# The first microseconds of a fused layernorm, state-space and gated feed-forward kernel: first tile loaded in halves, parameters on another queue, transposed tiles evicted in halves

## The chip, the cores and the metric

The kernel runs on one core of a Trainium2 chip. The metric is device time in microseconds; 179.80 is the median of three runs of the kernel before. One execution was also profiled; "the profile" is the page made of it and "the trace" is what can be asked of it beyond the page. The names of the engines are those of the profile: PE is TensorE's matmuls and PEld its weight loads, DVE is VectorE, ACT is ScalarE, POOL is GpSimd, SP is SyncE, which here only issues DMAs. ScalarE issues a few DMAs as well.

## The reference

The input x has 2048 tokens of 512 channels. Three things are summed:

```python
xn = _layernorm(x, axis=-1)
return x + _A_ref(xn, ...) + _B_ref(xn, ...)

# _A_ref: a diagonal complex state-space layer with 512 states
dt = jnp.exp(log_dt)
Lam_bar = jnp.exp(dt * Lam)
B_bar = ((Lam_bar - 1.0) / Lam)[:, None] * Bmat
Bu = jnp.einsum("bld,pd->blp", x + 0j, B_bar)
h = Lam_bar[None, :] * h + Bu[:, t, :]          # over all tokens t
y = 2.0 * jnp.einsum("blp,dp->bld", hseq, Cmat).real + x * Dskip[None, None, :]

# _B_ref: a gated feed-forward layer, 512 -> 1376 -> 512
return (_gelu(x @ w_gate) * (x @ w_up)) @ w_down
```

All inputs and the output are bf16.

## The kernel before

The 2048 tokens are 16 tiles of 128 and 4 blocks of 512. A tile has its 128 tokens on the partitions. It is normalised (statistics, then "centring": subtract the mean, multiply by the reciprocal root) and then transposed, so that channels lie on the partitions for the matmuls. In block 0, "the lead", TensorE transposes: four 128x128 transposes for a tile go into one PSUM bank (`TR_lead`, L594), and ScalarE copies the bank into the transposed array XNT, called its eviction (L597). Tile 0 alone is centred, transposed and evicted in two halves of two transposes each. The other blocks are transposed by DMA (`TR`, L640).

TensorE's work then is, block by block: gate and up projections (`gu_mm`, L772, on 128 rows of the hidden dimension at a time; `lead_gates_first`, L608, and `lead_mm` do the first two such row groups tile by tile in the lead), the state-space input B (`bu_mm`, L715), the down projection (L846) and the state-space output C (L857), which adds to the same bank. The state-space recurrence runs on VectorE: the input is rotated by tables of sines and cosines (L743 to L748), scanned (L754) and rotated back (`CHAIN`).

The decay parameters log_dt, Lambda_re and Lambda_im are three loads of 1 KB (`ld_param`, L475). Each is transposed on TensorE (`TR_par`, L617), and ScalarE takes the exponentials and copies from the PSUM bank it went to (`decay`, L653 to L659); VectorE makes the phases of these (L660 to L665) and the tables' arguments (L670 to L674).

Statistics of the lead's tiles are two VectorE operations (L530, L531). The reciprocal root is two ScalarE operations for tiles 0, 1 and 3 (L565, L566) and two GpSimd operations for tile 2 (L550, L551). `LN_lead` pins VectorE's order: statistics of tiles 0 and 1, both half centrings of tile 0 (L559), statistics of tile 2, and in between the centring of tile 1 (L546), then tile 3's statistics and the centrings of tiles 2 and 3.

Order of the work. Every operation is registered with the buffers that it reads and writes and an estimated duration. TensorE and SyncE run their operations in the order of registration. For VectorE, ScalarE and GpSimd a list scheduler picks the order by estimated times and due times, except for what `S.pin` fixes: pinned operations of an engine come first, in the order given. Waits are then generated: every operation waits for the semaphores of what it depends on, and an engine runs strictly in its order. A DMA issue is an operation of the engine that issues it.

Before any data is there, TensorE runs filler matmuls (`warm_pe`, L873): two of 128 columns and eight of 512, and one of 128 between tile 0's transposes and the first gate matmuls. The lead's order on TensorE and the pinned order on ScalarE are these:

```python
evT = [TR_lead(0)]
TR_par(0)
TR_par(1)
warm_pe(1, 128, 3)
lead_gates_first()
evT.append(TR_lead(1))
lead_mm((0, 1), 0, 1, (1,))
lead_mm((0,), 1, 2)
evT.append(TR_lead(2))
...
S.pin(*prm, g0, u0, ldln, *rs[0], *rs[1], *evT[0], exps[0], *evT[1], *rs[3], *evT[2], cps[1], *exps[1:3], *evT[3],
      *exps[3:], cps[0], gelu0)
```

ScalarE's queue thus issues log_dt, Lambda_re and the first columns of the gate and up weights (g0, u0) before it loads its first table (ldln). SyncE's queue issues the four lead tiles one by one, Lambda_im, the two transposing loads of B (L479), and the rest of the weights and tiles.

Of the kernel before, what the change touches and what calls it, by code (L numbers as in the profile page):

```python
# [9 lines left out]
ALU = mybir.AluOpType  # L10
# [308 lines left out]
def d_pe(n_list):  # L319
    return sum(max(62.0, n / 2.4 + 2.5) for n in n_list)  # L320
# [10 lines left out]
def build(nc, ins, out):  # L331
    with ExitStack() as es:
# [175 lines left out]

        POOL(lambda e: e.memset(NHALF.ap, -0.5), 100, [], [NHALF], "const")
        POOL(lambda e: e.memset(EPS.ap, EPS_LN), 100, [], [EPS], "const")  # L510
        POOL(lambda e: e.iota(IOT.ap, [[1, 128]], base=0, channel_multiplier=-1), 300, [], [IOT], "iota")
        POOL(lambda e: e.iota(IOTJ.ap, [[1, 512]], base=0, channel_multiplier=0), 600, [], [IOTJ], "iotj")
        ZWs = [Buf("ZWa", "sb", ZW.lo, ZW.lo + 256, ZW.ap[:, 0:128]), Buf("ZWb", "sb", ZW.lo + 256, ZW.hi, ZW.ap[:, 128:512])]
# [11 lines left out]

        GATE = {"gelu": []}

        def stats(tt):
            b, j = divmod(tt, 4)
            return [V(lambda e: e.bn_stats(ST[tt].ap, X[tt].ap), 640, [X[tt]], [ST[tt]], "bnst", slack=4000.0),  # L530
                    V(lambda e: e.bn_aggr(MVt[b][j].ap, ST[tt].ap), 100, [ST[tt]], [MVt[b][j]], "bnag", slack=4000.0)]  # L531
# [17 lines left out]
        def rsqrt(dst, var, r, n):  # L549
# [4 lines left out]
                for h in range(2)]  # L554
        XNT0h = [Buf("XNT0h%d" % h, "xnt", 0.5 * h, 0.5 * (h + 1)) for h in range(2)]

# [44 lines left out]

        def lead_gates_first():
            for h in range(2):
                def f(e, h=h):
                    ins_ = None
                    for dk in range(2 * h, 2 * h + 2):
                        for k in range(2):
                            ins_ = e.matmul(PS[2 * k][:, 0:128], WG.ap[:, dk, 128 * k:128 * k + 128], XNT[0].ap[:, dk, 0:128],  # L608
                                            start=(dk == 0), stop=(dk == KD - 1))
                    return ins_  # L610
                PE(f, d_pe([128] * 4), [WGc[0], XNT0h[h]], [bank_part(2 * k, 0, 512) for k in range(2)], "GU0")

        PPB = (5, 5, 4)
        PP = [PSH[PPB[i]][:, KP * i:KP * (i + 1)] for i in range(3)]

# [3 lines left out]
        def LN(b, on_act=True):  # L619
            for tt in range(4 * b, 4 * b + 4):  # L620
                sums(tt) if on_act else stats(tt)
            if on_act:
                rsqrt(RQb[b], SSQb[b].ap, [SSQb[b]], 4)
                POOL(lambda e: e.tensor_scalar(NRQb[b].ap, SUMb[b].ap, -1.0 / D, None, ALU.mult), 250, [SUMb[b]], [NRQb[b]], "nrq")
                POOL(lambda e: e.tensor_tensor(NRQb[b].ap, NRQb[b].ap, RQb[b].ap, ALU.mult), 1500, [NRQb[b], RQb[b]], [NRQb[b]], "nrq")  # L625
            else:
                rsqrt(RQb[b], MV[b].ap[:, :, 1], [MV[b]], 4)
            for j in range(4):
                tt = 4 * b + j
# [4 lines left out]
                else:  # L634
                    center(tt)

# [15 lines left out]
        def decay():  # L652
            exps = [ACT(lambda e: e.activation(DTB.ap, PP[0], ACTF.Exp), 200, [BANK[5]], [DTB], "exp_dt")]  # L653
            for s in range(KP):
                exps.append(ACT(lambda e, s=s: e.activation(PA[RRr].ap[:, s:s + 1], PP[1][:, s:s + 1], ACTF.Exp,
                                                            scale=DTB.ap[:, s:s + 1]),
                                200, [BANK[5], DTB], [A.sub(PA[RRr], "RR_%d" % s, s)], "exp_a"))
            c = [ACT(lambda e: e.activation(LRE.ap, PP[1], ACTF.Copy), 200, [BANK[5]], [LRE], "par"),
                 ACT(lambda e: e.activation(LIM.ap, PP[2], ACTF.Copy), 200, [BANK[4]], [LIM], "par")]  # L659
            d = [V(lambda e: e.tensor_tensor(pa(TH), DTB.ap, LIM.ap, ALU.mult), D_TINY, [DTB, LIM], [PA[TH]], "th"),  # L660
# [73 lines left out]
        def CHAIN(b):  # L734
# [146 lines left out]
        def preload(tag, fn=lambda e: e.preload_act_table(ACTF.Gelu_apprx_tanh)):  # L881
# [120 lines left out]
```

## Time and profile before

| | |
|---|---|
| median of three runs | 179.80 us (179.71 to 180.05) |
| the profiled execution | 179.66 us |
| its span, first to last instruction | 177.9 us |
| TensorE busy | 174.1 us, 98% of the span |
| VectorE busy | 161.8 us, 91% |
| ScalarE busy | 103.5 us, 58% |
| GpSimd busy | 9.5 us, 5% |
| first filler matmul, first transposes, first B matmul | 0.98, 4.90, 10.62 us |

A line of the chain is "start us, us, what": the chain is followed back from the last instruction, at each step to what released it or to the instruction before it on its engine. A line of a timeline is "start us, us, engine line op out<-in xcount [idle before <-releaser]", where neighbours of one line are merged. The time of a matmul in a group's row contains its drain; where matmuls follow each other, the distance of their starts is the time that each costs. A line of DMA issues ends with the us from issue to landing. Times of single instructions and packets are read from the same trace.

### The profile page before, as it was taken

The page shows a single profiled execution, that of the slowest core. Times are in us where ns is not written, and L with a number is a line of the kernel's source. Part 1 is how long each engine was busy: PE and PEld are TensorE (multiplying, and loading weights), DVE is VectorE, ACT ScalarE, POOL GpSimd, SP SyncE. Part 2 cuts the span into 40 slices and gives each one's busy share as a digit, 9 for nine tenths or more (in the row PEclk, how much of TensorE's full clock was granted, in tenths as well). Part 3 has the DMA queues.
Part 4 walks back from the last instruction along what each step waited for, and adds up shares of the span by engine and source line. Part 5 has one row for each costly group of instructions (what it writes and reads, how often), then busy time and mean ns, then how long its engine had stood idle before and what let it go on. Part 6 is the DMA issues. An engine that isn't in the chain of part 4 may idle for free.

```text
span 177.9 us, 2417 instructions
## 1 busy us (share of the span) xinstructions
PE 174.1 (98%) x881; PEld 81.9 (46%) x881; DVE 161.8 (91%) x249; ACT 103.5 (58%) x199; POOL 9.5 (5%) x21
## 2 busy tenths in 40 slices
PE   7999999999999999999999999999999999999994
PEld 2664444444444444444444444444444444444463
DVE  5799999998999989999999999999988999999631
ACT  3699999899998999396667500047867610000000
POOL 2100210000000601400000000000000000000000
PEclk9999999999999999999999999999999999999999
DMA  5999635995000022232000000110000000002020
GB/s 141 261 283 345 198 61 131 314 188 132 0 0 0 4 60 58 88 90 58 4 2 0 0 0 0 61 63 0 0 0 0 4 0 0 0 29 88 4 88 30
DMA packets 25267, 12.38 MB, mean 70 GB/s; under 512 B 15432, under 2 KB 25256, under 8 KB 25256
## 3 DMA queue, kind: packets, MB, share of 16 engines
q1 hardware_dynamic: 24184, 11.70, 25.6%
q10 hardware_dynamic: 1072, 0.53, 1.2%
q8 instruction: 7, 0.11, 0.2%
q14 instruction: 4, 0.03, 0.1%
HBM read 6.46 MB, written 2.10 MB: 48 GB/s over the span
## 4 chain that ended last, share of the span: by engine, by line
PE 95%; DVE 1%; DMA 1%; ACT 0%; issue 0%
PE PS L772 39%; PE PS L846 21%; PE PS L857 16%; PE PS L715 16%; PE PS L804 2%; DMA arena<-in_A_x_dram 1%; PE PS L820 1%; DVE arena L530 1%; PE PS L594 1%; PE PS L608 0%; ACT arena L597 0%; DVE arena L864 0%; DVE arena L531 0%; DVE arena L559 0%; PE PS L617 0%
## 5 line engine op out<-in xcount | busy, mean ns | idle before, releaser
L772 PE MATMUL PS<-arena 128*128 128x512 bf16 (+1 forms) x360 | 70.1, 354 | 0.1
L772 PEld LDWEIGHTS PS<-arena 128*128 128x128 bf16 x360 | 32.8, 98 | 36.6 <-ACT arena L811 0.8
L846 PE MATMUL PS<-arena 128*128 128x512 bf16 (+3 forms) x187 | 39.0, 366 | 0.0
L754 DVE TENSOR_TENSOR_SCAN arena<-arena 128x512 bf16<-128x512 f32 x32 | 38.6, 1251 | 0.0
L857 PE MATMUL PS<-arena 128*128 128x512 bf16 (+1 forms) x136 | 28.6, 366 | 0.0
L715 PE MATMUL PS<-arena 128*128 128x512 bf16 x128 | 28.3, 379 | 0.0
L780 ACT ACTIVATE arena<-PS 128x512 bf16<-128x512 f32 x40 | 23.8, 595 | 6.5 <-PE PS L772 4.9
L846 PEld LDWEIGHTS PS<-arena 128*128 128x128 bf16 (+1 forms) x187 | 18.3, 98 | 20.0
L724 ACT ACTIVATE arena<-PS 128x512 bf16<-128x512 f32 x26 | 15.1, 598 | 20.0 <-PE PS L715 19.9
L782 ACT ACTIVATE arena<-PS 128x512 bf16<-128x512 f32 x40 | 23.9, 596 | 4.9 <-PE PS L772 4.5
L857 PEld LDWEIGHTS PS<-arena 128*128 128x128 bf16 x136 | 13.3, 98 | 14.4
L715 PEld LDWEIGHTS PS<-arena 128*128 128x128 bf16 x128 | 12.5, 98 | 14.8
L784 DVE TENSOR_TENSOR arena<-arena 128x512 bf16<-128x512 bf16 x40 | 16.2, 420 | 2.9 <-ACT arena L782 2.2
L743 DVE TENSOR_TENSOR arena<-arena 128x4096 bf16<-128x4096 bf16 x8 | 18.3, 2286 | 0.1
L744 DVE TENSOR_TENSOR arena<-arena 128x4096 bf16<-128x4096 bf16 x8 | 18.3, 2283 | 0.0
L864 DVE TENSOR_TENSOR arena<-PS,arena 128x512 bf16<-128x512 f32 (+1 forms) x17 | 10.8, 652 | 6.6 <-PE PS L857 6.3
L834 DVE TENSOR_TENSOR arena<-arena 128x512 f32<-128x512 bf16 x16 | 10.8, 689 | 0.4
L745 DVE TENSOR_TENSOR arena<-arena 128x2048 bf16<-128x2048 bf16 x8 | 9.8, 1220 | 0.2
L631 ACT ACTIVATE arena<-arena 128x512 bf16<-128x512 bf16 x8 | 6.0, 803 | 2.5 <-POOL arena L625 2.5
L833 DVE TENSOR_TENSOR arena<-arena 128x512 bf16<-128x512 bf16 x16 | 6.4, 417 | 0.0
L530 DVE BATCH_NORM_STATS2 arena<-arena 128x6 f32<-128x512 bf16 x8 | 5.2, 680 | 1.1 <-DMA arena<-in_A_x_dram 1.1
L707 DVE SCALAR_TENSOR_TENSOR arena<-arena 128x512 bf16<-128x512 bf16 x8 | 5.7, 745 | 0.3 <-ACT arena L705 0.3
(74 smaller groups left out, 101.6 us busy)
## 6 DMA issues: line engine op xcount, KB each, us to landing
out_dram<-arena SPq DMA_DIRECT2D x15, 128.0 KB, 1.7
arena<-in_A_x_dram SPq DMA_DIRECT2D x3, 512.0 KB, 7.2
arena<-in_B_w_down_dram SPq DMA_DIRECT2D x1, 1280.0 KB, 6.8
arena<-in_B_w_gate_dram SPq DMA_DIRECT2D x2, 384.0 KB, 6.4
arena<-in_B_w_up_dram SPq DMA_DIRECT2D x2, 384.0 KB, 7.0
arena<-in_A_x_dram SPq DMA_DIRECT2D x4, 128.0 KB, 2.8
arena<-in_B_w_gate_dram SPq DMA_DIRECT2D x1, 352.0 KB, 8.5
arena<-in_B_w_up_dram SPq DMA_DIRECT2D x1, 352.0 KB, 7.9
```

Of the source, the lines that this page charges most:

```text
L715: ins_ = e.matmul(PS[bank][:, c0:c1], BBT[c].ap[:, dk, 128 * s:128 * (s + 1)], XNT[b].ap[:, dk, c0:c1], start=(dk == 0), stop=(dk == KD - 1))
L724: return ACT(lambda e: e.activation(ss.ap, PS[bank][:, :], ACTF.Copy), d_act(512), [BANK[bank]], [ss], "evBu", slack=1500.0)
L743: V(lambda e: e.tensor_tensor(TB.ap, ssb.ap, sin4, ALU.mult), d_dve_tt2x(4096), [ssb, SINT], [TB], tag)
L744: V(lambda e: e.tensor_tensor(TA.ap, ssb.ap, cos4, ALU.mult), d_dve_tt2x(4096), [ssb, COST], [TA], tag)
L754: V(lambda e, g=g, rb=rb, init=init: e.tensor_tensor_scan(g.ap, rb, g.ap, init, ALU.mult, ALU.add), d_dve_scan(512), [g, PA[RRr]] + ([CARc ...
L772: ins_ = e.matmul(PS[bank][0:m, c0:c1], W.ap[:, dk, 128 * ft:128 * ft + m], XNT[b].ap[:, dk, c0:c1], start=(dk == 0), stop=(dk == KD - 1))
L780: g = ACT(lambda e: e.activation(GG[kk].ap[0:m, :], PS[bg][0:m, :], ACTF.Gelu_apprx_tanh), d_act(512), [BANK[bg]], [GG[kk]], "gelu", after ...
L782: u = ACT(lambda e: e.activation(UPB[kk].ap[0:m, :], PS[bu][0:m, :], ACTF.Copy), d_act(512), [BANK[bu]], [UPB[kk]], "evU", slack=1500.0)
L784: h = V(lambda e: e.tensor_tensor(HTt[k2][ft].ap[0:m, :], GG[kk].ap[0:m, :], UPB[kk].ap[0:m, :], ALU.mult), d_dve_tt2x(512), [GG[kk], UPB[ ...
L834: V(lambda e: e.tensor_tensor(XD[tt % 4].ap, X[tt].ap, XN[tt].ap, ALU.add), d_dve_1x(512), [X[tt], XN[tt]], [XD[tt % 4]], "xd")
L846: ins_ = e.matmul(o_, HTt[k2][ft].ap[0:m, tok], WD.ap[0:m, ft, c0:c1], start=(ft == 0), stop=False)
L857: ins_ = e.matmul(o_, SSc[k3][s][c].ap[:, tok], CT[c][s].ap[:, c0:c1], start=False, stop=(s == KP - 1 and c == 1))
```

## The change

The first x tile is loaded as two halves of 64 rows: the upper one, with a new name X0B, is the first issue of ScalarE's queue, and the lower one the first of SyncE's; tile 0's statistics wait for both. The three parameter loads move to GpSimd's queue, and GpSimd's start is pinned: the small iota, two constants, the three loads, then the large iota. VectorE's pinned order puts the centring of tile 1 before the statistics of tile 2.

In the lead, tile 1 and tile 2 are now transposed into two banks and evicted in halves, as tile 0 was (tile 3 still goes whole), and a new function `lead_half` does the gate and up matmuls of a tile for one half of the channels, so that they need one half of the eviction. The three parameter transposes go behind tile 2's transposes, all into bank 7. The filler is seven and a half long matmuls instead of eight, and 256 columns instead of 128 in the second place. ScalarE's pinned order follows the new order. Last, the two products of the first rotation must come after the centring of block 1, which is registered before `CHAIN(0)`.

```diff
-        prm = [ld_param(T_, nm, "scalar") for T_, nm in ((PRM[0], "A_log_dt"), (PRM[1], "A_Lambda_re"))]
+        X0B = Buf("X0B", "x0b", 0, 1)
+        x0b = load(X[0].ap[64:128, :], x2[64:128, :], 64 * 1024, [X0B], "ld_x", "scalar")
+        load(X[0].ap[0:64, :], x2[0:64, :], 64 * 1024, [X[0]], "ld_x")
         g0 = ld_w(WG, WGc, ins["B_w_gate"], 0, "scalar")
         u0 = ld_w(WU, WUc, ins["B_w_up"], 0, "scalar")
-        for t in range(4):
+        for t in range(1, 4):
             ld_x(t, 1)
-        ld_param(PRM[2], "A_Lambda_im")
...
+        S.pin(POOL(lambda e: e.iota(IOT.ap, [[1, 128]], base=0, channel_multiplier=-1), 300, [], [IOT], "iota"),
+              POOL(lambda e: e.memset(EPS.ap, EPS_LN), 100, [], [EPS], "const"),
+              POOL(lambda e: e.memset(NHALF.ap, -0.5), 100, [], [NHALF], "const"),
+              *[ld_param(T_, nm, "gpsimd") for T_, nm in ((PRM[0], "A_log_dt"), (PRM[1], "A_Lambda_re"), (PRM[2], "A_Lambda_im"))],
+              POOL(lambda e: e.iota(IOTJ.ap, [[1, 512]], base=0, channel_multiplier=0), 600, [], [IOTJ], "iotj"))
...
-            S.pin(*st[0], *st[1], *ln[0], st[2][0], *ln[1], st[2][1], *st[3], *ln[2], *ln[3])
+            S.pin(*st[0], *st[1], *ln[0], *ln[1], *st[2], *st[3], *ln[2], *ln[3])
...
         def TR_lead(tt):
-            if tt:
-                bank = 6 + tt % 2
-                parts = [(bank, XN[tt], XNTt[tt], 0, KD)]
+            banks = ((6, 7), (6, 7), (4, 5), (6, 6))[tt]
+            if banks[0] == banks[1]:
+                parts = [(banks[0], XN[tt], XNTt[tt], 0, KD)]
             else:
-                parts = [(6 + h, XN0h[h], XNT0h[h], 2 * h, 2 * h + 2) for h in range(2)]
+                parts = [(banks[h], XN0h[h] if tt == 0 else XN[tt], XNTh[tt][h], 2 * h, 2 * h + 2) for h in range(2)]
...
+        def lead_half(t, h, which=(0, 1)):
+            c0, c1 = 128 * t, 128 * t + 128
+
+            def f(e):
+                ins_ = None
+                for dk in range(2 * h, 2 * h + 2):
+                    for k in range(2):
+                        for i in which:
+                            ins_ = e.matmul(PS[2 * k + i][:, c0:c1], (WG, WU)[i].ap[:, dk, 128 * k:128 * k + 128],
+                                            XNT[0].ap[:, dk, c0:c1], start=(dk == 0), stop=(dk == KD - 1))
+                return ins_
+            PE(f, d_pe([128] * 4 * len(which)), [(WGc, WUc)[i][0] for i in which] + [XNTh[t][h]],
+               [bank_part(2 * k + i, 4 * c0, 4 * c1) for k in range(2) for i in which], "GU0")
...
-        PPB = (5, 5, 4)
+        PPB = (7, 7, 7)
...
-                V(lambda e: e.tensor_tensor(TB.ap, ssb.ap, sin4, ALU.mult), d_dve_tt2x(4096), [ssb, SINT], [TB], tag)
-                V(lambda e: e.tensor_tensor(TA.ap, ssb.ap, cos4, ALU.mult), d_dve_tt2x(4096), [ssb, COST], [TA], tag)
+                V(lambda e: e.tensor_tensor(TB.ap, ssb.ap, sin4, ALU.mult), d_dve_tt2x(4096), [ssb, SINT], [TB], tag, after=GATE["rot"])
+                V(lambda e: e.tensor_tensor(TA.ap, ssb.ap, cos4, ALU.mult), d_dve_tt2x(4096), [ssb, COST], [TA], tag, after=GATE["rot"])
...
         warm_pe(2, 128)
-        warm_pe(8)
+        warm_pe(7)
+        warm_pe(1, 256)
         evT = [TR_lead(0)]
-        TR_par(0)
-        TR_par(1)
-        warm_pe(1, 128, 3)
-        lead_gates_first()
+        warm_pe(1, 256, 3)
+        lead_half(0, 0, (0,))
+        lead_half(0, 1, (0,))
         evT.append(TR_lead(1))
-        lead_mm((0, 1), 0, 1, (1,))
-        lead_mm((0,), 1, 2)
+        lead_half(0, 0, (1,))
+        lead_half(0, 1, (1,))
+        lead_half(1, 0)
+        lead_half(1, 1)
         evT.append(TR_lead(2))
-        TR_par(2)
+        for i in range(3):
+            TR_par(i)
         exps, cps, dec, t3 = decay()
-        lead_mm((1,), 1, 2)
+        lead_half(2, 0)
         evT.append(TR_lead(3))
-        lead_mm((0, 1), 2, 3)
+        lead_half(2, 1)
...
-        S.pin(*prm, g0, u0, ldln, *rs[0], *rs[1], *evT[0], exps[0], *evT[1], *rs[3], *evT[2], cps[1], *exps[1:3], *evT[3],
-              *exps[3:], cps[0], gelu0)
+        S.pin(x0b, g0, u0, ldln, *rs[0], *rs[1], *evT[0], *evT[1], *rs[3], *evT[2], exps[0], cps[1], *evT[3],
+              *exps[1:], cps[0], gelu0)
...
         factor()
+        GATE["rot"] = LN(1, False)
         CHAIN(0)
-        LN(1, False)
+        GATE["rot"] = []
```

More of the change, by code (lines that the diff above doesn't have):

```diff
@@ L507, in late_loads @@
             ld_x(12, 4)
[L509 to L512, printed above, removed]
+        S.pin(POOL(lambda e: e.iota(IOT.ap, [[1, 128]], base=0, channel_multiplier=-1), 300, [], [IOT], "iota"),
[3 more added lines that the diff above has]
+              POOL(lambda e: e.iota(IOTJ.ap, [[1, 512]], base=0, channel_multiplier=0), 600, [], [IOTJ], "iotj"))
         ZWs = [Buf("ZWa", "sb", ZW.lo, ZW.lo + 256, ZW.ap[:, 0:128]), Buf("ZWb", "sb", ZW.lo + 256, ZW.hi, ZW.ap[:, 128:512])]
@@ L524, in next_bank @@
             return b_
-        GATE = {"gelu": []}
+        GATE = {"gelu": [], "rot": []}
         def stats(tt):
             b, j = divmod(tt, 4)
-            return [V(lambda e: e.bn_stats(ST[tt].ap, X[tt].ap), 640, [X[tt]], [ST[tt]], "bnst", slack=4000.0),
+            return [V(lambda e: e.bn_stats(ST[tt].ap, X[tt].ap), 640, [X[tt]] + ([X0B] if tt == 0 else []), [ST[tt]], "bnst", slack=4000.0),
                     V(lambda e: e.bn_aggr(MVt[b][j].ap, ST[tt].ap), 100, [ST[tt]], [MVt[b][j]], "bnag", slack=4000.0)]
@@ L554, in build @@
                 for h in range(2)]
-        XNT0h = [Buf("XNT0h%d" % h, "xnt", 0.5 * h, 0.5 * (h + 1)) for h in range(2)]
+        XNTh = [[Buf("XNTh%d_%d" % (t, h), "xnt", t + 0.5 * h, t + 0.5 * (h + 1)) for h in range(2)] for t in range(4)]
         def center_half(h):
@@ L600, in TR_lead @@
             return ev
[L602 to L611, printed above, removed]
-        PPB = (5, 5, 4)
+        def lead_half(t, h, which=(0, 1)):
[11 more added lines that the diff above has]
+        PPB = (7, 7, 7)
         PP = [PSH[PPB[i]][:, KP * i:KP * (i + 1)] for i in range(3)]
@@ L627, in LN @@
                 rsqrt(RQb[b], MV[b].ap[:, :, 1], [MV[b]], 4)
+            cs = []
             for j in range(4):
@@ L634, in LN @@
                 else:
-                    center(tt)
+                    cs.append(center(tt))
+            return cs
         def TR(b):
@@ L652, in decay @@
         def decay():
-            exps = [ACT(lambda e: e.activation(DTB.ap, PP[0], ACTF.Exp), 200, [BANK[5]], [DTB], "exp_dt")]
+            exps = [ACT(lambda e: e.activation(DTB.ap, PP[0], ACTF.Exp), 200, [BANK[7]], [DTB], "exp_dt")]
             for s in range(KP):
@@ L656, in decay @@
                                                             scale=DTB.ap[:, s:s + 1]),
-                                200, [BANK[5], DTB], [A.sub(PA[RRr], "RR_%d" % s, s)], "exp_a"))
-            c = [ACT(lambda e: e.activation(LRE.ap, PP[1], ACTF.Copy), 200, [BANK[5]], [LRE], "par"),
-                 ACT(lambda e: e.activation(LIM.ap, PP[2], ACTF.Copy), 200, [BANK[4]], [LIM], "par")]
+                                200, [BANK[7], DTB], [A.sub(PA[RRr], "RR_%d" % s, s)], "exp_a"))
+            c = [ACT(lambda e: e.activation(LRE.ap, PP[1], ACTF.Copy), 200, [BANK[7]], [LRE], "par"),
+                 ACT(lambda e: e.activation(LIM.ap, PP[2], ACTF.Copy), 200, [BANK[7]], [LIM], "par")]
             d = [V(lambda e: e.tensor_tensor(pa(TH), DTB.ap, LIM.ap, ALU.mult), D_TINY, [DTB, LIM], [PA[TH]], "th"),
```

## The prediction

> **What bounds the kernel.** I read the totals first, then the chain that ended last in order of time, then each engine's timeline for the first 11 us. Totals and chain shares:
>
> ```profile
> PE 174.1 (98%) x881; PEld 81.9 (46%) x881; DVE 161.8 (91%) x249; ACT 103.5 (58%) x199; POOL 9.5 (5%) x21
> PE 95%; DVE 1%; DMA 1%; ACT 0%; issue 0%
> ```
>
> TensorE is busy 98% of the span, and the chain is TensorE for 95%. The chain in order of time (start us, us, what) shows where the rest lies:
>
> ```profile
> 0.73 2.04 DMA arena<-in_A_x_dram
> ...
> 2.79 0.71 DVE arena L530
> ...
> 3.70 0.59 DVE arena L530
> ...
> 4.50 0.36 DVE arena L559
> ...
> 4.90 0.54 PE PS L594 x4
> ...
> 6.36 0.24 PE PS L594 x4
> ...
> 6.62 0.61 ACT arena L597
> ...
> 7.27 0.62 PE PS L772 x8
> 7.89 0.22 PE PS L594 x4
> ...
> 8.22 0.55 PE PS L772 x8
> 8.77 0.22 PE PS L594 x4
> 8.99 1.79 PE PS L772 x32
> 10.78 6.91 PE PS L715 x32
> ```
>
> From 7.27 us to 175.40 every piece is TensorE, and each starts where the last ends. 32 matmuls of 512 columns take 6.91 us, 0.216 each; 32 of 128 columns 1.79, 0.056 each. No pause is left behind 7.27, so nothing there can be shortened by waiting less. The change can move the time only through the moment at which the first B matmul (L715) starts, 10.62 in the timeline (the chain counts 0.16 later), or by making a new pause. The useful work starts with the first transposes (L594) at 4.90: the stretch to judge is 4.90 to 10.62, 5.72 us.
>
> **The sum's base.** The profiled execution took 179.66 us: a span of 177.9 and 1.76 around it. The median shown is 179.80, 0.14 more; the runs lie within 0.34. About 0.2% (0.36 us) is what a measurement tells from no change.
>
> **First tile in two halves.** The x tile's 128 KB went out at 0.73 and had landed at 2.77. A 1 KB parameter on the scalar queue, issued at 0.73 too, landed at 2.06: no halving beats that, so the gain lies between 0 and 0.71. Packets of the tile run from 1.74 to about 2.3, and both halves cross the same 16 DMA engines, where each 1 KB packet takes 0.046 us and an engine has eight (0.37). I take 0.12, nearer to zero because only the ragged end of that 0.56 can go. Downstream it is passed on in full only while tile 1 keeps up: VectorE does both tiles' statistics (L530, L531) before the first centring (L559), the second starts at 3.62, and tile 1 landed at 3.30. That caps the gain at 0.32, or near 0.5 if tile 1's own issue (1.18) comes 0.2 sooner behind a shorter first one.
>
> **Scalar queue.** Two parameter issues (0.55 and 0.26) go, one half tile (between 0.26 and 0.55) comes: gate and up weights and the table load come about 0.4 sooner. The table load ended at 3.92 and the first rsqrt step followed at 3.93; that step would now wait on VectorE (3.70), but the centring at 4.50 waits on VectorE's second aggregate (ends 4.495) anyway: 0. The up weights landed at 6.45, and TensorE waited for them from 6.41 to 6.50: this 0.08 goes.
>
> **Sync queue.** One parameter issue (0.45) goes; the B transposes and all weight loads behind come about 0.5 sooner. The first B matmul's operand landed at 8.50 and was needed at 10.62, so 0.
>
> **Filler.** Seven and a half long matmuls for eight: 0.21 less, hidden while the first transposes wait for VectorE (filler ended near 4.58, transposes at 4.90). The second filler, 256 columns for 128, lies in the pause before 5.72: 0.
>
> **Lead order on TensorE**, with the first transposes still at 4.90:
> - Gates of tile 0 end at 6.19, as before; the two parameter transposes that left this place stood in the wait for the eviction.
> - Tile 1's centring now precedes tile 2's statistics: VectorE can start it at 5.09 instead of 5.71. Its transposes stay at 6.19, since TensorE is busy until then. Ups of tile 0: 6.41 to 6.86.
> - Tile 1's eviction in halves. A half took 0.38 (L597, 128x256), a whole 0.60. The second transpose is issued at 6.25, drains in 0.22, ScalarE starts 0.03 later: 6.50 to 6.88; the matmul follows 0.05 behind: 6.94, where it was 7.27. Sixteen matmuls to 7.83.
> - Tile 2: its statistics start at 5.42 behind the centring (its data landed at 5.07), aggregate ends 6.33, GpSimd's two steps (0.09 wait, 0.32, 0.58) end at 7.31, centring 7.35 to 7.76. TensorE comes at 7.83: no wait. Transposes to 8.06, three parameter transposes (0.17, from 0.13 for two) to 8.23. The first half's eviction: 7.89 + 0.22 + 0.03 = 8.14, to 8.53, matmul at 8.58. **TensorE pauses 0.35.**
> - Eight matmuls to 9.03, tile 3's transposes to 9.25, eight matmuls to 9.70. Tile 3 is evicted whole: last transpose issued 9.20 + 0.22 + 0.03 = 9.45, + 0.60 = 10.05, matmul at 10.10. **TensorE pauses 0.40**: eight matmuls (0.45) cover this eviction, where before sixteen did (8.83 to 9.72) and no pause was left.
> - Sixteen matmuls: first B matmul at 11.00.
>
> So 6.10 for 5.72: pauses of 0.31 and 0.08 are exchanged for 0.07, 0.35 and 0.40: +0.38. Bounds: were an eviction worth only its pitch in a row (0.28 a half, 0.48 a whole), the two pauses lose 0.10 and 0.12: +0.16. Were the matmul to follow as late as behind the first eviction (5.60 to 5.75, 0.15 for 0.05), they gain 0.1 each: +0.58. I keep 0.38, tile 1's own row.
>
> **Parameters on GpSimd.** Its two steps for tile 2 are wanted at 6.33 and the three transposes at 8.06; the large iota (0.56) goes behind the three issues. The trace has no DMA of this engine. Lower bound: the issues elsewhere, 0.26 to 0.55, which end before 2.8. Upper: a transpose issue, 3.04 each, to 10.2. The nearest rows are the same 1 KB loads, so I take 0.55 and zero cost; the cover is 5.3 us less 0.56.
>
> **Rotation held.** Before, the centring of block 1 (L546) is at 22.61 and the first rotation product (L743) at 24.58: the order is already so. Held behind it are that product, the next (2.28 each) and the scans; TensorE wants their result at 68.0, and it was ready at 58.5. Without this order four transposes (5.12 on SP from 23.05, landing near 29.6) could pass 32.2, where the B matmuls of block 1 want them. Zero, cover 2.6.
>
> **Behind the lead.** ScalarE reaches the gelu table load 0.8 later (10.01 to about 10.8). Banks 4 and 5 are freed at 14.35, wanted at 17.5; then near 22, wanted at 24.6. VectorE's phase chain starts at 9.15 instead of 8.84, its bank 6 copy near 16.3, wanted at 19.3. Covers over 1.7 us: 0.
>
> **Sum:** 179.66 + 0.38 - 0.12 = 179.92, or 180.06 against the median. I forecast 180.0, no change that can be told, on the slow side.
>
> **Rivals.**
> 1. *Tile 1 lands late.* Gate weights are issued 0.4 sooner, near 1.2, right at tile 1's issue. For it: tile 2, issued 0.04 behind the gate weights, took 3.4 us to land, tile 1 2.1. Against: tile 1 still goes first by about 0.1. It decides past 3.6. Landing like tile 2, at 1.1 + 3.4 = 4.5, it delays the first centring by 0.9: 180.95.
> 2. *Parameters late.* TensorE runs in order, so everything behind the transposes at 8.06 waits. Lambda_im took 3.94 to land, issued at 2.66: if that holds, issues over 1.0 us each (8.06 - 3.94 - 1.06, by three) are too long. At 1.3 each the stop is 0.9, partly over the pause of 0.35: 180.6. Against: early small loads landed in 1.3 to 1.5. The Trainium skill (SBUF — State Buffer, "SBUF: two separate sides") says that VectorE's two-port operations lock GpSimd out of writing descriptors for a DMA of its queue; one that takes 0.62 us alone took 3.1 beside a copy. By it the rival's time holds or is passed, at up to three times 3.1; no row here shows it.
> 3. *TensorE stays at half pace.* The filler runs at 0.43 per 512 columns, later matmuls at 0.216. The pace changes near 4.8, and the filler would stop 0.2 sooner, leaving 0.42 idle instead of 0.32 before the transposes. If that keeps the slow pace, forty 128-column matmuls cost 0.05 more each, 2.0, less 0.4 of pauses: 181.6. Against: the pause hardly grows. The Trainium skill (TensorE: Matmul & The Clock Gate, "What's actually happening") names the mechanism, activity in a window of 3.4 us at a free-running phase; the trace agrees that 3.8 us of filler passed before full pace.
> 4. *Faster.* The first tile gains the capped 0.5 and the pauses before tiles 2 and 3 shrink to the lower value, +0.16: 179.32, or 179.46 against the median, with the spread of the runs (0.34) on both sides of it. For it: two queues fetch side by side, and packets began slowly (41 in the first quarter us, 69 in the next). It decides when the gain passes the pauses' growth by 0.36.
>
> **Chances.** Forecast 0.45 (own range 179.7 to 180.4; 0.32 within 0.2%, 0.13 slower). Rival 1 0.15, rival 2 0.12, rival 3 0.05: slower. Faster rival 0.23, half of it (0.12) beyond 0.2%, 0.11 within. Together faster 0.12, same 0.43, slower 0.45. The range runs from 179.4 into rival 1's price, 181.0: about 0.1 is left below, 0.1 above.
>
> **What would show it.** The first transposes near 4.8; tile 1's first matmul near 6.8; pauses of about 0.35 and 0.40 ended by ScalarE's L597 behind the transposes of tiles 2 and 3; the first B matmul near 10.9; TensorE without a pause behind it. It is wrong if the first transposes start before 4.5 or after 5.1, if a parameter's landing ends a TensorE wait, or if a pause appears after the lead.

## The result and the profile after

The changed kernel took 182.02 us in the median of six runs (180.65 to 182.56), the kernel before 179.84 (179.71 to 180.05): a ratio of 1.0104, 95% interval 1.0061 to 1.0147. It is slower; the forecast was 180.0, no change that can be told, and its range ended at 181.0.

The runs fall into two groups, which the profile of a single execution cannot show. With six further runs of the same kernel (experiment 8) twelve are known: five at 180.65 to 181.07 and seven at 181.71 to 182.56, 1.5 us apart by their medians (180.82 and 182.36); the one at 181.71 stands alone between them. The profiled execution, 180.65 us with a span of 178.8, is of the lower group. So there are two losses to explain: about 1 us that every run has, and 1.5 us that seven of twelve have on top.

The totals of the profile after:

```profile
PE 173.2 (97%) x866; PEld 81.8 (46%) x881; DVE 161.0 (90%) x249; ACT 103.6 (58%) x201; POOL 11.4 (6%) x24
PE 94%; DMA 1%; DVE 1%; ACT 1%; issue 1%
```

TensorE is still the bound. Fifteen of its 881 matmul records are missing, so positions are taken from weight loads, which are all there. The chain in order of time (start us, us, what), up to the first B matmuls (L722 here; transposes are L596, evictions L599, half-tile matmuls L612):

```profile
0.74 2.52 DMA arena<-in_A_x_dram
3.29 0.70 DVE arena L532
...
5.28 0.30 PE PS L596 x2
...
6.13 0.61 PE PS L612 x8
6.74 0.22 PE PS L596 x4
7.00 1.51 PE PS L612 x24
8.51 0.17 PE PS L596 x2
8.71 0.39 ACT arena L599
...
9.14 0.62 PE PS L612 x8
9.76 0.24 PE PS L596 x4
10.02 0.61 ACT arena L599
10.68 1.07 PE PS L779 x16
...
11.80 6.85 PE PS L722 x31
```

The x tile now ends its load at 3.26 instead of 2.77, and the first transposes start at 5.28 instead of 4.90. Tile 1's matmuls follow those of tile 0 without a break (24 in one piece; the forecast had a pause of 0.07), but from 7.00. Then ScalarE's eviction stands in the chain twice, behind the transposes of tile 2 (8.71) and of tile 3 (10.02): the two pauses that the prediction described. The first weight load of the B matmuls is at 11.53, before at 10.56, 0.96 later by the unrounded times. From there to the last weight load it is 164.44 us in both kernels, equal to the hundredth. Everything happened in the lead, and the span grew by the same 0.97.

ScalarE's DMA queue in the kernel after, and the same two weight issues in the kernel before (start us, us, engine line op):

```profile
0.74 0.57 ACTq L463 DMA_DIRECT2D arena<-in_A_x_dram  x1
1.34 0.86 ACTq L463 DMA_DIRECT2D arena<-in_B_w_gate_dram  x1
2.23 0.53 ACTq L463 DMA_DIRECT2D arena<-in_B_w_up_dram  x1
```

```profile
1.60 0.44 ACTq L463 DMA_DIRECT2D arena<-in_B_w_gate_dram  x1
2.08 0.53 ACTq L463 DMA_DIRECT2D arena<-in_B_w_up_dram  x1
```

A half of 64 rows took 0.57 us to issue on each queue, where the whole tile of 128 rows took 0.39 on one; and the gate weights behind it took 0.86 for 0.44. The up weights went out at 2.23, later than before (2.08), and landed at 6.95 instead of 6.45: TensorE waited 0.2 for them at 7.00.

### The profile page after: what moved, and what is told of

Its sections match the earlier page's. It is cut to its first block, busy times and chain, and to the rows that moved or that the text cites. A ratio compares the mean times of both kernels' runs of the same rounds, so it can differ in the third digit from the quotient of the medians.

```text
span 178.8 us, 2406 instructions
## 1 busy us (share of the span) xinstructions
PE 173.2 (97%) x866; PEld 81.8 (46%) x881; DVE 161.0 (90%) x249; ACT 103.6 (58%) x201; POOL 11.4 (6%) x24
## 4 chain that ended last, share of the span: by engine, by line
PE 94%; DMA 1%; DVE 1%; ACT 1%; issue 1%
PE PS L779 37%; PE PS L853 21%; PE PS L864 15%; PE PS L722 15%; PE PS L811 2%; PE PS L612 2%; DMA arena<-in_A_x_dram 1%; PE PS L827 1%; ACT arena L599 1%; DVE arena L532 1%; PE PS L596 1%; DVE arena L871 0%; DVE arena L533 0%; DVE arena L561 0%
## 5 line engine op out<-in xcount | busy, mean ns | idle before, releaser
L779 PE MATMUL PS<-arena 128*128 128x512 bf16 (+1 forms) x313 | 67.0, 371 | 0.6 <-ACT arena L599 0.2
L779 PEld LDWEIGHTS PS<-arena 128*128 128x128 bf16 x320 | 30.5, 98 | 36.6 <-ACT arena L818 0.8
L864 PE MATMUL PS<-arena 128*128 128x512 bf16 (+1 forms) x136 | 28.6, 366 | 0.0
L722 PE MATMUL PS<-arena 128*128 128x512 bf16 x124 | 27.6, 379 | 0.2
L864 PEld LDWEIGHTS PS<-arena 128*128 128x128 bf16 x136 | 13.3, 98 | 14.4
L722 PEld LDWEIGHTS PS<-arena 128*128 128x128 bf16 x128 | 12.5, 98 | 14.8
```

What stands on the lines that cost most here:

```text
L722: ins_ = e.matmul(PS[bank][:, c0:c1], BBT[c].ap[:, dk, 128 * s:128 * (s + 1)], XNT[b].ap[:, dk, c0:c1], start=(dk == 0), stop=(dk == KD - 1))
L779: ins_ = e.matmul(PS[bank][0:m, c0:c1], W.ap[:, dk, 128 * ft:128 * ft + m], XNT[b].ap[:, dk, c0:c1], start=(dk == 0), stop=(dk == KD - 1))
L864: ins_ = e.matmul(o_, SSc[k3][s][c].ap[:, tok], CT[c][s].ap[:, c0:c1], start=False, stop=(s == KP - 1 and c == 1))
```

## The experiments

Each ran against the kernel before on the same chip; the medians of before were 179.97 (beside 1, 3, 7, 8), 179.83 (2, 4, 9, 10), 179.97 (5, 6, 12) and 179.83 (11, 13). Three chips were used, which the record numbers: chip 0 for experiments 1, 3, 7 and 8, chip 10 for 2, 4, 9, 10, 11 and 13, chip 9 for 5, 6 and 12. Two single runs far outside, 652.85 us in experiment 4 and 309.77 us in experiment 13 (at a mean granted clock of 0.56), are left out. Positions are those of the one traced run of each kernel.

| run | first transposes | first B weight load | up weights land | times of its runs |
|---|---|---|---|---|
| before | 4.90 | 10.56 | 6.45 | 179.69 to 180.32; four of 90 at 181.3 to 181.7 |
| after | 5.28 | 11.53 | 6.95 | 180.65 to 182.56 |
| lead_alone | 4.90 | 11.15 | 6.48 | 180.20 to 180.73, 182.21, 182.53 |
| lead_long_filler | 4.90 | 11.18 | 6.66 | 180.15 to 180.67 |
| whole_tile | 5.81 | 12.07 | 5.39 | 181.17, 181.23, 182.57, 182.73 |
| table_first | 5.78 | 12.04 | 5.90 | 180.92 to 181.17, 182.15, 182.45 |
| loads_alone | 5.17 | 11.49 | 7.31 | 180.04 to 180.69, 181.89 |
| params_sync | 5.24 | 11.62 | 7.08 | 180.60 to 181.07, 182.19, 182.20, 182.44 |

**1, 2. The lead alone** (lead_alone, lead_long_filler). All loads as before, with the changed order, evictions and filler; in the second the filler is longer by one long matmul.

```diff
 # lead_alone, against after
-        x0b = load(X[0].ap[64:128, :], ...)
+        prm = [ld_param(T_, nm, "scalar") for T_, nm in ((PRM[0], "A_log_dt"), (PRM[1], "A_Lambda_re"))]
...
 # lead_long_filler, in addition
-        warm_pe(7)
+        warm_pe(8)
         warm_pe(1, 256)
```

> The lead of the changed kernel (order, halved evictions, filler, parameter transposes behind tile 2) with all loads as in the kernel before. The prediction's step for the lead: pauses of 0.35 and 0.40 us for 0.31 and 0.08, first transposes at 4.90, first B matmul at 11.00, +0.38: 180.2. Theory C (the filler is 0.2 us shorter, so the clock can stay low): the spread of up to 1.9 us is here too. Theories H and P: the spread is gone, below 0.4 us.

> The changed lead with the loads of before, whose runs were 180.20 to 180.73 with two of ten at 182.2 and 182.5; here with eight and a half long filler matmuls instead of seven and a half (ending near 4.8, first transposes at 4.9). Theory C: no run over 181, median about 180.4, which is the price of the lead's order alone, first B matmul at 11.15 against 10.56. Theory L: one run in five at 182.2 or more.

Measured: 180.50 and 180.42, the second at a ratio of 1.0029 (1.0019 to 1.0039), +0.59 in medians and +0.62 in the B matmul's start. TensorE's timeline of lead_long_filler:

```profile
6.70 1.51 PE L610 MATMUL PS<-arena 128*128 128x128 bf16 x24
8.80 0.62 PE L610 MATMUL PS<-arena 128*128 128x128 bf16 x8 [0.21 <-ACT arena L597]
9.48 0.61 PE L610 MATMUL PS<-arena 128*128 128x128 bf16 x8
10.34 1.07 PE L777 MATMUL PS<-arena 128*128 128x128 bf16 x16 [0.24 <-ACT arena L597]
```

Each drain of a matmul counts as busy here, so a pause in brackets reads shorter than the distance of starts. From the last matmul before 10.34 (9.48 plus eight times 0.056) it is 0.41, forecast 0.40. The missing 0.2 lies ahead of tile 2's transposes, which the prediction had at 7.83. In this trace the up weights landed at 6.66, the 24 matmuls start at 6.70 instead of 6.41, and the transposes come at 8.05. In lead_alone's trace the weights landed at 6.48 and the matmuls start at 6.53, and still the transposes come at 8.00 (TensorE's timeline, then VectorE's):

```profile
6.53 1.51 PE L610 MATMUL PS<-arena 128*128 128x128 bf16 x24
8.00 0.40 PE L594 MATMUL PS<-arena 128*128 128x128 bf16 x4
```

```profile
5.29 0.41 DVE L546 TENSOR_SCALAR arena<-arena 128x512 bf16<-128x512 bf16 x1 [0.18 <-ACT arena L566]
7.53 0.41 DVE L546 TENSOR_SCALAR arena<-arena 128x512 bf16<-128x512 bf16 x1 [0.22 <-POOL arena L551]
```

The 24 matmuls were through at 7.87 (24 times 0.056 behind 6.53), and the transposes waited for the centring of tile 2 (L546), which ended at 7.95 and not at the 7.76 of the prediction. The centring of tile 1, ahead of tile 2's statistics, waited for ScalarE's reciprocal root (L566) and started at 5.29, forecast 5.09; all that follows moved with it. In lead_long_filler tile 1's started at 5.19 and tile 2's ended at 7.85, under the cover of the late weights. So up weights on time would not have brought the forecast 0.4: with the transposes 0.06 behind the centring as in lead_alone, so between 7.91 and 8.00, the lead's price is between 0.46 and 0.55, an estimate from these ends. The two runs above 182 in lead_alone, and none in lead_long_filler, belong to experiments 8 to 11.

**3, 4, 5. The loads of the lead** (whole_tile, halves_alone, table_first).

```diff
 # whole_tile, against after: one load of 128 rows on SyncE; ScalarE's queue starts with the gate weights
-        x0b = load(X[0].ap[64:128, :], ...)
-        load(X[0].ap[0:64, :], ...)
-        for t in range(1, 4):
+        for t in range(4):
...
 # halves_alone, against before: halves; the parameters stay on ScalarE's queue behind the half
+        x0b = load(X[0].ap[64:128, :], x2[64:128, :], 64 * 1024, [X0B], "ld_x", "scalar")
+        load(X[0].ap[0:64, :], x2[0:64, :], 64 * 1024, [X[0]], "ld_x")
...
 # table_first, against whole_tile: order on ScalarE, filler of eight and a half
-        S.pin(g0, u0, ldln, ...
+        S.pin(ldln, g0, u0, ...
```

> The changed kernel with the first tile loaded whole on SyncE's queue, as before; the rest stays changed. Theory H: the first transposes return to about 4.9 us (from 5.28) and up weights, now first on ScalarE's queue, land near 5.9, so the first B matmul comes near 11.0 and the time is 0.4 to 0.6 us less than the changed kernel's fastest, about 180.1, with a spread below 0.4. Theories P and C: the fastest run gains 0.4 too, but the spread of up to 1.9 us stays.

> The kernel before with the first tile in two halves on two queues, and the parameter issues kept behind the half on ScalarE's queue, so that the weights are issued no sooner than before. The prediction's step: the second half lands 0.12 sooner than the whole tile (2.77), first transposes at 4.78. Theory H1 (two issues at once slow each other): the second half lands near 3.2 here too and the first transposes come near 5.2, time 180.1 to 180.3, with some runs near 182 by theory C since the pause before the transposes grows to 0.6. Theory H2 (the weights, issued 0.3 us sooner, take the DMA engines from the half): here it lands near 2.7 and the first transposes stay at or under 4.9.

> The changed kernel with the tile loaded whole and ScalarE's table load put ahead of its two weight issues, which then go out near 2.0 us, behind tile 1's (1.2); eight and a half long filler matmuls. With the weights first, tile 1 landed at 4.59 and the first transposes came at 5.81. Rival 1 of the prediction (the gate weights hold tile 1 back): tile 1 lands near 3.3 and the first transposes return to 4.9; the up weights land near 6.8, and the time is near 180.5 in every run. If something else of the changed loads holds tile 1 back, it stays at 4 or later and the transposes after 5.2.

whole_tile did the opposite of what was expected: 181.9 in the median, the first transposes at 5.81. VectorE's timeline shows which wait did it:

```profile
3.32 0.69 DVE L529 BATCH_NORM_STATS2 arena<-arena 128x6 f32<-128x512 bf16 x1 [1.99 <-DMA arena<-in_A_x_dram]
4.61 0.69 DVE L529 BATCH_NORM_STATS2 arena<-arena 128x6 f32<-128x512 bf16 x1 [0.38 <-DMA arena<-in_A_x_dram]
5.44 0.57 DVE L558 TENSOR_SCALAR arena<-arena 128x256 bf16<-128x256 bf16 x2
```

Without the half ahead of them the gate weights went out at 0.73, tile 1 at 1.18 behind them, and tile 1 landed at 4.59 instead of 3.30; both tiles' statistics stand ahead of the first centring (L558). That is the prediction's first rival at its own price: 0.9 later. Tile 0 came late as well: whole, on its queue of before, it landed at 3.30 instead of 2.77 with the weights' issue beside it, as late as the second half (3.26). So the whole tile was no return to the kernel before, and this run cannot say what the halves cost. It does show that two issues which start together need not take longer: the whole tile's took 0.40 and the gate weights' 0.46, both from 0.73. table_first was meant to hold the weights back, but the table load did not hold ScalarE's queue:

```profile
0.73 1.28 ACT L890 ACT_TABLE_LOAD   x1 [0.73 <-PEq L995]
0.76 0.45 ACTq L463 DMA_DIRECT2D arena<-in_B_w_gate_dram  x1
```

So it repeats whole_tile: tile 1 at 4.55, transposes at 5.78, 180.9 to 181.2 in eight of ten runs. The contrary is in the runs that issue the gate weights behind tile 1 (1.60 in before, 1.62 in lead_alone and lead_long_filler): tile 1 at 3.30 to 3.58. In the changed kernel the two issues go out together (1.34 and 1.36) and tile 1 usually just wins: 3.53 and 3.98 in two traces.

halves_alone (181.61, 181.82, 182.00) agrees with theory H1 for the landing and not with H2: with the weights held back to 2.66 the second half still landed at 3.20, and both issues took 0.56. H1's reason, that two issues at once slow each other, is not shown: whole_tile's did not. The first transposes, expected at 5.2, came at 5.92, because five issues ahead of the table load moved that to 3.66 to 4.94, and the first rsqrt step behind it to 4.95. And its traced run was at half pace until 9.86 (see 8 to 11). So its time is no measure of the halves alone.

**6. All loads, the lead of before** (loads_alone).

```diff
 # against before: x0b and the lower half, parameters on gpsimd, weights behind x0b
-        warm_pe(8)
+        warm_pe(9)
+        warm_pe(1, 128)
```

> The lead's order of before with all loads of the changed kernel (halves on two queues, parameters from GpSimd, weights behind the half), and nine and a half long filler matmuls, so that the clock plays no part. Theory H (the two first issues slow each other, and tile 1 and the up weights follow later): first transposes near 5.25 us where tile 1 lands by 3.6, up weights near 6.95, first B matmul 10.9 to 11.0, 180.2 to 180.3; where tile 1 is served behind the gate weights it lands near 5.0 and the run takes 181.0. If the loads cost nothing, 179.8.

Measured: 180.38, +0.41 on the medians of ten runs, though the ratio's interval (0.9978 to 1.0042) holds 1: one run is at 181.89, and four of the 29 runs of before beside it are above 181.3. The traced run, 180.64, had the first transposes at 5.17, as expected, and the up weights only at 7.31. Loads (+0.41) and lead (+0.59) add up to +1.00.

**7. The parameters** (params_sync). The three loads go to SyncE's queue behind tile 3; no DMA is issued from GpSimd.

```diff
-              *[ld_param(T_, nm, "gpsimd") for T_, nm in (...)],
+        for T_, nm in ((PRM[0], "A_log_dt"), (PRM[1], "A_Lambda_re"), (PRM[2], "A_Lambda_im")):
+            ld_param(T_, nm)
```

> The changed kernel with the three parameter loads on SyncE's queue behind tile 3, where no DMA is issued from GpSimd; the halves and the lead stay changed. Theory P: the spread falls below 0.4 us and the time is near the changed kernel's fastest, 180.6. Theory H: no change of the spread, since the halves are still there, 180.6 to 182.5. Theory C: no change of the spread either.

Measured: 180.76, three of nine runs above 182, first B weight load at 11.62 against 11.53. The lower group is where the changed kernel's is, and the upper one is still there: GpSimd's queue costs nothing. Its issues in the kernel after:

```profile
1.39 0.77 POOL L475 DMA_DIRECT2D arena<-in_A_log_dt_dram  x1 [0.25 <-issue]
2.17 0.53 POOL L475 DMA_DIRECT2D arena<-in_A_Lambda_re_dram  x1
2.69 0.52 POOL L475 DMA_DIRECT2D arena<-in_A_Lambda_im_dram  x1
```

One took 0.77 and two the 0.5 that was taken, and the last parameter landed at 7.22, 1.5 before the parameter transposes (8.71).

**8 to 11. The two groups** (after_again, before_short_filler, after_long_filler, after_5_filler). The changed kernel again, and three kernels that differ from one of the two compared in nothing but the filler ahead of the first transposes.

```diff
 # before_short_filler, against before
-        warm_pe(8)
+        warm_pe(7)
+        warm_pe(1, 256)
 # against after (7 long and one of 256): after_long_filler       after_5_filler
-        warm_pe(7)
-        warm_pe(1, 256)
+        warm_pe(9); warm_pe(1, 128)                              # or: warm_pe(5)
```

> The changed kernel once more, for a second trace and more times: its six runs lie between 180.65 and 182.56 us, the kernel before's six between 179.71 and 180.05. Theory H (the halves arrive late): the first transposes stay near 5.3 us and the runs differ by when the halves land. Theory P (parameters on GpSimd's queue): where a run is long, TensorE waits at the three parameter transposes (near 8.5 us) for a landing. Theory C (clock): where a run is long, matmuls of the lead run at 0.107 us per 128 columns instead of 0.056. All three expect times between 180.6 and 182.6; the trace should show which wait is longer than in the first one.

> The kernel before with nothing changed but the filler of the changed kernel (seven and a half long matmuls, ending near 4.36 instead of 4.58, first transposes at 4.9). Theory C: most runs at 179.8 to 180.2 and some, one or two in ten, at 181.7 to 182.3, which the kernel before never showed in 26 runs. Theory L: all runs between 179.7 and 180.3.

> The changed kernel with two more long filler matmuls (nine of 512 columns and one of 128, ending near 5.13 instead of 4.36), so that TensorE pauses 0.1 instead of 0.9 us before the first transposes. Theory C (a pause before the first transposes keeps TensorE at half pace for another 3.4 us in some runs): the upper group of times, 181.6 to 182.7, is gone and all runs lie between 180.5 and 181.1. Rival theory L (in the long runs a DMA of the lead lands late): the two groups, 180.6 to 181.1 and 182.1 to 182.5, stay as they are.

> The changed kernel with five long filler matmuls instead of seven and a half: the filler ends near 3.3 us and TensorE pauses 1.9 us before the first transposes at 5.2. Theory C: now most runs are in the upper group, 181.8 to 182.8, and a trace of one shows 128-column matmuls 0.107 us apart (0.056 at full pace) past 6.5 us. If the filler's length plays no part, the runs stay split as before, 180.6 to 181.1 and 182.1 to 182.5, and the trace shows full pace before 6 us.

after_again: 180.82 to 182.43, both groups, but its trace fell in the lower one and told nothing of the upper. before_short_filler: eight runs at 179.72 to 180.32 and two at 181.36 and 181.38, one of them traced. TensorE's timeline in it:

```profile
4.88 0.65 PE L594 MATMUL PS<-arena 128*128 128x128 bf16 x4 [0.32 <-DVE arena L559]
7.08 1.93 PE L772 MATMUL PS<-arena 128*128 128x128 bf16 x16
10.52 1.95 PE L772 MATMUL PS<-arena 128*128 128x128 bf16 x32
```

Sixteen matmuls of 128 columns take as long at 7.08 as thirty-two at 10.52. The trace's record of the granted clock turns full at 10.27 in this run; in the kernel before it did so at 4.82. All loads landed as before. after_5_filler: all four runs in the upper group, 181.69 to 182.62, and its traced run shows the same in the changed kernel, with full pace from 11.46:

```profile
5.20 0.65 PE L596 MATMUL PS<-arena 128*128 128x128 bf16 x4 [1.70 <-DVE arena L561]
7.40 2.77 PE L612 MATMUL PS<-arena 128*128 128x128 bf16 x24
```

2.77 for 24 matmuls that take 1.51 in the kernel after. A third trace at half pace is that of halves_alone, with the filler of before and first transposes at 5.92; its record turns full at 9.86:

```profile
8.11 1.90 PE L775 MATMUL PS<-arena 128*128 128x128 bf16 x16
10.96 1.95 PE L775 MATMUL PS<-arena 128*128 128x128 bf16 x32
```

after_long_filler: 180.81, 180.87, 180.93 and 181.62. No run is above 182, and the fourth has another cause that its trace shows: tile 1 landed at 5.03 there, VectorE waited 0.95 for it, and the first transposes came at 6.25, the first rival again. So theory C holds for the upper group and L falls for it: after a pause behind the filler TensorE can stay at half pace. It need not: the traced runs of whole_tile and after_long_filler paused 1.24 and went on at full pace. How often, beside the pause that the profile shows before the first transposes (0.11 in the kernel before from 4.79 to 4.90):

| kernel | pause in its traced run | runs above 181.2, without those that a late tile explains |
|---|---|---|
| before | 0.11 | 4 of 90 |
| lead_v2 (filler as before) | 0.13 | 2 of 12 |
| lead_long_filler, lead_v2_fill (filler to 4.8) | none | 0 of 21 |
| loads_alone (filler to 5.1) | none | 1 of 10 |
| before_short_filler | 0.32 | 2 of 10 |
| lead_alone | 0.61 | 2 of 10 |
| params_sync | 0.67 | 3 of 9 |
| after and after_again | 0.70, 0.63 | 7 of 12 |
| table_first | 0.78 | 2 of 10 |
| halves_alone | 1.14 | 3 of 3 |
| whole_tile | 1.24 | 2 of 4 |
| after_5_filler | 1.70 | 4 of 4 |

The order is not strict over all runs. The run of loads_alone and the 181.71 of the changed kernel may be late tiles, which put a run at 181.62 in experiment 10; neither was traced. Within a chip the order is clearer. On chip 10 it is 0 of 35 for the kernel before, 0 of 21 without a pause, 2 of 10 at 0.32, 3 of 3 at 1.14 and 4 of 4 at 1.70; on chip 0 it is 0 of 20 for the kernel before and 10 of 29 for the four kernels with pauses from 0.61 to 1.24. Chip 9 is the exception: the four of the kernel before are all among its 29 runs there, and lead_v2's two are there too. What makes it differ was not looked into.

The recorded clock of the untraced runs points the same way. Of all runs near 180 us four have a mean granted clock of 0.991, the others 0.999 or 1.0, and the four are long ones: 182.36 and 182.56 of the changed kernel, 182.44 of params_sync, 182.00 of halves_alone. Half pace for 3.3 us of 181 would give 0.991, an estimate. The record does not show every such stretch: the traced run of before_short_filler, at half pace until 10.27, has 1.0, since its record starts where the clock turns full.

**12, 13. A lead with the pauses covered** (lead_v2, lead_v2_fill). Loads, filler and VectorE's order as before; tiles 1 and 2 evicted in halves, but tile 3's transposes and the parameter transposes moved ahead of tile 2's matmuls. The second adds 256 columns of filler.

```diff
 # against lead_alone
-            S.pin(*st[0], *st[1], *ln[0], *ln[1], *st[2], *st[3], *ln[2], *ln[3])
+            S.pin(*st[0], *st[1], *ln[0], st[2][0], *ln[1], st[2][1], *st[3], *ln[2], *ln[3])
...
-        warm_pe(7)
-        warm_pe(1, 256)
+        warm_pe(8)
...
         evT.append(TR_lead(2))
+        evT.append(TR_lead(3))
         for i in range(3):
             TR_par(i)
         exps, cps, dec, t3 = decay()
         lead_half(2, 0)
-        evT.append(TR_lead(3))
         lead_half(2, 1)
```

> All loads, the filler and VectorE's order as in the kernel before; of the change only the halved evictions of tiles 1 and 2, with tile 3's transposes and the parameter transposes moved ahead of tile 2's matmuls, so that sixteen matmuls cover tile 3's eviction. By the step for the lead: tile 1's matmuls from 6.95 to 7.9, transposes of tiles 2 and 3 to 8.4, parameters to 8.6, tile 2 from 8.65, tile 3 from 9.55, first B matmul at 10.45 against 10.56: 0.1 less than before, 179.7. If the pauses before tiles 2 and 3 are not what the lead's order cost, it stays near 180.4.

> The lead with the two pauses covered (179.69 to 180.22 in ten runs, two more at 181.5), and the filler longer by 256 columns, ending near 4.8 beside first transposes at 4.9. Theory C: no run over 180.6, median 179.85, 0.1 less than the kernel before's undisturbed runs. If the filler plays no part, one run in six at 181.5 again.

Measured: lead_v2 179.84 in the median, ten runs at 179.69 to 180.22 and two at 181.5, ratio 0.9997 (0.9968 to 1.0027); lead_v2_fill 180.02 over its eleven, 179.64 to 180.45, ratio 1.0009 (1.0000 to 1.0019). This lead gives the loss back and beats the changed kernel, but not the one before; the 0.1 expected cannot be told. How much of it is the covered pauses and how much VectorE's order, which went back with them, these runs do not separate. In lead_v2's trace the two pauses are gone (it is of the slowest of the ten, 180.22: its up weights landed at 7.22 and the 24 matmuls start at 7.27):

```profile
9.37 1.07 PE L610 MATMUL PS<-arena 128*128 128x128 bf16 x16
10.27 1.06 PE L777 MATMUL PS<-arena 128*128 128x128 bf16 x16
```

## Why the prediction was wrong

The place was right: only the lead moved, and from the first B matmul on the kernels are equal (164.44 us). So were the pauses that the lead's order makes, forecast 0.35 and 0.40. The prediction's own sign of being wrong, first transposes after 5.1, came true (5.28). The lower group's 180.82 lies inside the range, but not by the working of the sum: the range ends at 181.0 for rival 1, which the two traces of that group do not show. The steps put at zero behind the lead, the held rotation and the parameters on GpSimd stayed at zero, the last two within their stated covers. Four steps failed.

- **"First tile in two halves": taken as a gain of 0.12, measured a loss of 0.50 in the landing (2.77 to 3.26) and 0.38 at the first transposes.** The bounds were 0 and 0.71; a loss was excluded without a reason. The row that spoke for one was there: two issues at 0.73, one on each queue, of which ScalarE's took 0.55 for four rows of 256 bytes. The packets of the second half start 0.29 behind those of the first (2.37 and 2.08), and even the first half's start 0.34 later than the whole tile's did (1.74). The Trainium skill (SBUF — State Buffer, "Can I just issue two DMAs to hit both halves?") says that two such DMAs go one after the other and gain some 6%; the trace agrees on the order, with the last packet of the first half starting at 2.43, the first of the second at 2.37 and the halves landing at 2.87 and 3.26, but there was no gain: it was a loss. whole_tile shows that starting together is not enough to slow an issue (0.40 and 0.46); why the halves' took 0.57 is open.
- **"Scalar queue": weights 0.4 sooner, 0.08 saved.** The up weights went out 0.15 later (2.23 for 2.08), since the half's issue and the gate weights' behind it were both slowed, and landed 0.50 later. The wait of 0.08 became 0.2. With the late tile this is the loads' share: +0.41 alone.
- **"Lead order": +0.38, measured +0.59.** The two pauses held; the start of tile 2's transposes, 7.83, was the wrong term. They came at 8.05 behind up weights that landed at 6.66 (lead_long_filler), and at 8.00 behind tile 2's centring, which ended at 7.95 and not at 7.76 (lead_alone). The prediction took "no wait" there because it had tile 1's centring start at 5.09; it started at 5.19 in one trace and, behind ScalarE's root, at 5.29 in the other. A slip besides: the pauses that the prediction lists differ by 0.43, its times by 0.38, and it does not say what the 0.05 between them is.
- **Rival 3, the clock: given a chance of 0.05.** Its price was right (1.5 to 1.6 over the forecast, measured 1.5 between the groups) and its argument, "the pause hardly grows", was wrong: a shorter filler and a later first tile made it 0.70 where it was 0.11, by the ends in the profile (the prediction, which leaves out the drain, had 0.42 and 0.32). Six or seven of twelve runs paid. The step looked at the pause with the transposes at 4.78 and not at 5.28. This decides the median: without it, the three runs of after_long_filler at 180.81 to 180.93 have a median of 180.87, inside the range.

Rival 1 is a mechanism of this kernel with the predicted price (experiments 3, 5 and one run of 10), but in the changed kernel the tile mostly wins the race. Rival 2 is refuted by experiment 7. The faster rival needed a gain of the first tile that had the wrong sign.

How far the +0.41 of the loads splits between the late half and the late up weights was not separated: no kernel has the one without the other at the old queue order. No trace was caught of the long runs of the changed kernel itself; that they are at half pace rests on the three traces of other kernels, on the recorded clock of two of these runs (0.991), and on their going and coming with the filler.

## What to carry to other kernels

Before splitting a small first load over two queues, measure the two halves beside each other: here they took longer to issue and landed later than one load of twice the size, and everything behind them on both queues moved too. In a lead where filler holds TensorE's pace, the filler must reach the first real work: whoever delays that work or trims the filler has to look at many runs, since one profile shows only one of the outcomes. When a transpose is followed by its eviction, count the matmuls that lie between it and its first reader; splitting the eviction is worth less than one more group of matmuls in between.

## What was not expected of the hardware

- Two DMA issues of 64 rows each, started at once on SyncE's and ScalarE's queues, took 0.57 us each; one of 128 rows took 0.39 beside a tiny one (before) and 0.40 beside the 512 rows of the gate weights, which took 0.46 (whole_tile).
- Tile 1, issued 0.01 to 0.04 us behind the 512 short rows of the gate weights, landed at 3.5 to 4.0 in five traces and at 5.03 in one. In the kernel after its first packet starts at 2.57, ahead of the gate weights' (3.08); in the late case at 3.05, behind theirs (2.64). Which of the two is served first is worth 1 us.
- A weight issue on ScalarE's queue did not wait for the table load ahead of it (0.73 to 2.01): it started at 0.76.
- The stretch at full clock is 174.08 us long where it starts early (3.9 to 5.6 us) and 170.67 where it starts late (9.9 to 11.5), in the twelve traces near 180 us that record it: the two differ by 3.41, and no start lies between 5.7 and 9.8. The Trainium skill (TensorE: Matmul & The Clock Gate, "What's actually happening") gives a free-running window of 3.4 us, and the traces agree in this: the two lengths are 51 and 50 times 3.413. So a filler that breaks off early is not paid for by degrees but in one piece or not at all.
